# Where the bit patterns of the dense weights are put together: a PSUM bank in place of SBUF, for 16 of 32 pieces

## The chip, the cores and the metric

The kernel runs on one core of a Trainium2 chip. The metric is the device time of one execution in microseconds (us), as a median over runs. The engines have their own instruction streams and meet through semaphores: TensorE (PE in the profile, with its weight loads as PEld), VectorE (DVE), ScalarE (ACT), GpSimd (POOL) and SyncE (SP), which issues most DMAs. Working memory is SBUF; TensorE writes its results to PSUM, which has eight banks of 512 fp32 values in each of 128 partitions, and VectorE and ScalarE can read and write PSUM too.

## What is computed

Three layers follow each other. The first is attention over q, k and v of shape (4, 8, 768, 64), where each query sees the 4 first keys and a window of 128 keys:

```
scores = scale * q @ k.T                 # keep = sink | in_window, else -1e9
a = exp(scores - max); a = a / (sum(a) + 1e-9)
x = a @ v                                # -> 3072 tokens x 512
```

The second is a dense layer; w_in is 512 x 2048 and w_out 2048 x 512:

```
h = x @ w_in
g = where(h >= 1, h, where(h <= -1, 0, (h + 1)**2 / 4))
y = g @ w_out
```

The third routes the 3072 tokens of y to 8 experts with 384 places each, in the order of their gate logits, and gives each token its expert's `relu(y @ w1[e]) @ w2[e]`. The weights of the dense layer arrive as 64-bit floats, everything that the kernel multiplies is 32-bit.

## The kernel before, in words

**Splitting.** Matrix products take operands of type fp32r, with fewer mantissa bits than fp32. So each operand is split into a high part and a low part (names ending in h and l), and each product is three passes: low x high, high x low and high x high.

**Weights.** The two dense matrices come in 16 pieces each. Piece f of w_in holds columns 128f to 128f + 127, and piece f of w_out the same rows. A piece is a DMA of 512 KB into a tile dr (two of them), in which each weight is a pair of 32-bit words. `decode` (L230) turns a piece into fp32 and then into its two parts:

1. L237, ScalarE: the sign of the high word as plus or minus a power of two, written into the place of the low part.
2. L239, VectorE: bits of the low word, shifted, into the tile df; 128 x 512 elements.
3. L242, VectorE: the high word, shifted, combined with what L239 left in df.
4. L243, ScalarE: the absolute value, in place.
5. L244, VectorE: times the sign; df now holds the fp32 weights.
6. L245, ScalarE: the high part. L246, GpSimd: df minus the high part, the low part.

The tile df has three buffers in SBUF; pieces 12 to 15 of w_out use the pool tag "ev" instead, with two buffers that other tiles share. For w_out there are two more steps: `gate_t` (L210) transposes the piece on TensorE into a bank (gp), ScalarE copies it to SBUF (gw, L216), and `gate_m` (L218) multiplies it by the router's weights (gg), which ScalarE and VectorE split (L225, L226).

**Dense layer.** For a block of 256 tokens and each f, `hid` (L625) makes 128 hidden rows (hp), takes the activation over VectorE (L640, L642) and ScalarE (L641), and splits it into gh (ScalarE, L643) and gl (GpSimd, L644). `proj` multiplies both by piece f of w_out (up, L657). `hid` of f needs piece f of w_in, `proj` of f needs piece f of w_out with its gate part.

**PSUM.** Hidden rows use a tag H with two banks, the three sums of `proj` use U0, U1 and U2, and the tag A has two banks and R one. That makes eight. Transposes and scores ask `bank` (L179) for a bank; it goes round a list `free` of tags, which is A, A, R from plan time T0M on. So each third request gets the single bank R.

**Order.** `Plan` (L1340) collects steps, each with a time of the plan (about, but not exactly, microseconds), and then runs them in that order; this gives the instructions their priority, and the order on each engine is written when the program is built, by priority and by when inputs and buffers are expected to be free. The engines follow the written order. Pieces 0 to 6 of both matrices come at plan times 6 to 48; pieces 7 to 15 of w_in at D1 = 69 and every 2.79 after it; pieces 7 to 15 of w_out at 71.25 and every 4.5. The attention of block 2 begins at TA2 = 100. Blocks 0 and 1 of the dense layer, for which the weights must be decoded, run beside this.

Of the kernel before, what the change touches and what calls it, by code (L numbers as in the profile page):

```python
# [7 lines left out]
F32 = mybir.dt.float32  # L8
# [3 lines left out]
I32 = mybir.dt.int32  # L12
AF = mybir.ActivationFunctionType
OP = mybir.AluOpType
# [11 lines left out]
P = 128  # L26
# [19 lines left out]
H1, D0, DA, D1, DD = 7, 6.0, 6.5, 69.0, 4.5  # L46
# [5 lines left out]
TA2, TA3 = 100.0, 148.0  # L52
# [22 lines left out]
class Kernel:  # L75
# [154 lines left out]
    def decode(self, raw, oh, ol, late=False, pinned=False):  # L230

        nc = self.nc
        hw, lw = raw[:, :, :, 1], raw[:, :, :, 0]
        f = (self.mo if late else self.dec).tile([P, 4, P], F32, name="df", tag="ev" if late else "df", bufs=2 if late else 3)
        x, s = f.bitcast(I32), ol

        nc.scalar.activation(s, hw.bitcast(F32), AF.Sign, scale=2.0 ** -111 / 1.125)  # L237

        ins = nc.vector.tensor_scalar(x, lw, 29, 0x40000000, op0=OP.logical_shift_right, op1=OP.bitwise_xor)  # L239
        if pinned:  # L240
            self.tc.keep_in_program_order(ins)
        nc.vector.scalar_tensor_tensor(x, hw, 3, x, op0=OP.logical_shift_left, op1=OP.bitwise_xor)  # L242
        nc.scalar.activation(f, f, AF.Abs)  # L243
        nc.vector.tensor_tensor(out=f, in0=f, in1=s.bitcast(F32), op=OP.mult)  # L244
        nc.scalar.copy(oh, f)  # L245
        nc.gpsimd.tensor_tensor(out=ol, in0=f, in1=oh.bitcast(F32), op=OP.subtract)  # L246
        return f
# [1127 lines left out]
@with_exitstack  # L1375
def tile_sink_window_attention__moe__expert_choice(ctx, tc, q, k, v, n_sink, window, w_in, w_out, wg, w1, w2, out):
    a = dict(q=q, k=k, v=v, n_sink=n_sink, window=window, w_in=w_in, w_out=w_out, wg=wg, w1=w1, w2=w2, out=out)
    nc = tc.nc
    K = Kernel(ctx, tc, a)
    K.c = ctx.enter_context(tc.tile_pool(name="const", bufs=1))  # L1380
    dr = ctx.enter_context(tc.tile_pool(name="dr", bufs=1, space=DRAM))
    K.x2d = dr.tile([N, DM], F32, name="x2d")
    xg = dr.tile([B * H * S, D], F32, name="xg")
    K.logits = K.c.tile([P, B * NT, E], F32, name="logits")
    K.sk, K.sv, K.skf, K.svf = {}, {}, {}, {}

    def pipeline(general):
        with ExitStack() as c0:
            c1, c3, c4, cd = (c0.enter_context(ExitStack()) for _ in range(4))
            K.pools(c1.enter_context, c0.enter_context)  # L1390
            K.front_pools(c3.enter_context)
            K.dec = cd.enter_context(tc.tile_pool(name="dec", bufs=2, side="right"))
            if not general:
                K.consts()
            xs = {}
            gw, w_in, w_out, gate_t, gate_m = K.weight_steps()

            def xtiles(b):
                if b not in xs:
                    xs[b] = tuple(K.xp.tile([P, 4, TB], F32R, name=n, tag=n) for n in ("xh", "xl"))  # L1400
                return xs[b]

            def attn(plan, blks, t0, t1):
                if general:
                    for i, b in enumerate(blks):
                        plan.at(t0 + (t1 - t0) * i / len(blks), lambda b=b: K.load_x(b, xg, *xtiles(b)))
                    return
                steps = K.pipeline([p for b in blks for p in (K.attn_steps_f32 if b < NF else K.attn_steps)(b, xtiles)])
                dt = 1 / (len(steps) - 0.5)
                for i, s in enumerate(steps):  # L1410
                    plan.add(t0 + (t1 - t0) * dt * (i - 0.5 * (i > 0)), t0 + (t1 - t0) * dt * (i + 0.5), s)

            K.turn_, K.free = 0, ["U0", "A", "U1", "R", "U2", "A"]
            plan = Plan(tc)
            attn(plan, range(1), 0, T0A)
            attn(plan, range(1, 2), A1, B1)
            plan.at(T0M, lambda: setattr(K, "free", ["A", "A", "R"]))
            x01 = [xtiles(1), xtiles(0)]
            plan.add(T0M, T00, K.moe1_steps(0, lambda: xtiles(0), part=(0, H0)))
            plan.add(T1, T2, K.moe1_steps(1, lambda: xtiles(1)))  # L1420
            plan.add(T2, T3, K.moe1_steps(0, lambda: xtiles(0), part=(H0, FT)))
            plan.at(1, gw)
            if not general:
                plan.at(T0A, K.flags)

            def late():
                cd.close()
                K.late_weights(c1.enter_context)

            for f in range(FT):  # L1430
                t, TD = (D0 + f * DA, DA) if f < H1 else (D1 + (f - H1) * DD, DD)
                plan.at(t if f < H1 else D1 + (f - H1) * DD * WF, lambda f=f: w_in(f))
                if f == FA:
                    plan.at(t + TD / 2, late)
                plan.at(t + TD / 2, lambda f=f: w_out(f))
                plan.at(t + TD / 2 + TG, lambda f=f: gate_t(f))
                plan.at(t + TD / 2 + TG + (TH if f < FA - 1 else 1), lambda f=f: gate_m(f))

            def turn():
                c3.close()  # L1440
                K.router_pools(c0.enter_context)
                hold.append(c4.enter_context(tc.tile_pool(name="hold", bufs=1, side="right")))
                K.router_consts()
                K.rtag = "R"

            def clear():
                c4.close()
                c1.close()
                K.pools2(c0.enter_context)

            hold = []
            b1 = T3 + BLOCK * (NB - 3)
            attn(plan, range(2, 3), TA2, TA3)
            attn(plan, range(3, NB), TA3, b1 - BLOCK * AHEAD)
            for b in range(2, NB - 1):
                plan.add(T3 + BLOCK * (b - 2 - OV), T3 + BLOCK * (b - 1), K.moe1_steps(b, lambda b=b: xtiles(b)))
            plan.at(b1 - BLOCK * OV - 0.5, turn)
            to_logits, rest = K.moe1_steps(NB - 1, lambda: xtiles(NB - 1), lambda: hold[0])
            plan.add(b1 - BLOCK * OV, b1 + HB, to_logits)
            plan.add(b1 + HB, b1 + HB + TP, rest)  # L1460
            plan.at(b1 + HB + TP, clear)
            K.experts(plan, b1 + HB)
            plan.run()

    pipeline(False)
    flag = nc.values_load(K.flag[0:1, 0:1], min_val=0, max_val=1)
    with tc.If(flag):
        with ExitStack() as c0:
            K.attn_general(c0.enter_context, xg)
        pipeline(True)  # L1470
# [32 lines left out]
```

## Time and profile before

| | |
|---|---|
| median of 3 runs | 1175.04 us (1173.58 to 1175.45) |
| the profiled execution | 1172.83 us, of which the span from first to last instruction is 1171.0 |
| TensorE | 1102.2 us busy (94%), 8256 matmul records |
| weight loads of TensorE | 1017.4 us (87%) |
| VectorE | 872.2 us (74%) |
| ScalarE | 698.2 us (60%) |
| GpSimd | 487.0 us (42%) |
| mean granted TensorE clock | 0.982 of full speed |

"Busy" is the time in which an engine has an instruction running. A matmul's record overlaps the next one, so a busy TensorE is not TensorE at its peak. An idle time is put down to what released the waiting instruction, "<-"; it costs something only where the engine is the one that the end waits for. In the timeline rows a VectorE instruction's time overlaps its successor's by some 0.06 to 0.1 us.

### The profile page before, as it was taken

The numbers are of one execution on the slowest core, as the hardware profiler recorded it, in microseconds if no ns is written. First come the engines' busy times: TensorE is split into PE (matmuls) and PEld (weight loads), VectorE is DVE, ScalarE is ACT, GpSimd is POOL, SyncE is SP. The second block draws the span as 40 slices with busy tenths as digits, with TensorE's granted clock in tenths as the row PEclk, the third lists the DMA queues.
The fourth block names the chain that finished last, engine by engine and source line by source line (L and its number), as shares of the span: only waits on it lengthen the run. The fifth ranks groups of instructions, "written<-read, shape, count | busy, mean of one in ns | idle before, by whom it ended". The sixth has DMA issues, their size and how long they took to land.

```text
span 1171.0 us, 24367 instructions
## 1 busy us (share of the span) xinstructions
PE 1102.2 (94%) x8256; PEld 1017.4 (87%) x8256; DVE 872.2 (74%) x2718; ACT 698.2 (60%) x1598; POOL 487.0 (42%) x590
## 2 busy tenths in 40 slices
PE   5899888999999999999999999999799999999997
PEld 3688878999999999999999999999587788788896
DVE  5978978777777877776777787755788888788430
ACT  4887777566666666676667676643245445444552
POOL 1335745444545545455545554542213213322321
PEclk9899999999999999999999999999799999999999
DMA  4645522323222222223222222100485767667772
GB/s 105 173 143 158 158 60 61 70 42 64 53 39 56 36 55 49 61 46 64 34 54 49 58 46 56 22 19 1 120 228 168 204 180 216 188 194 202 217 218 66
DMA packets 241928, 118.13 MB, mean 101 GB/s; under 512 B 196096, under 2 KB 220672, under 8 KB 241792
## 3 DMA queue, kind: packets, MB, share of 16 engines
q1 hardware_dynamic: 231504, 85.36, 28.4%
q0 software_dynamic: 8592, 29.89, 10.9%
q8 instruction: 67, 1.10, 0.4%
q10 hardware_dynamic: 1696, 1.22, 0.3%
q14 instruction: 69, 0.57, 0.2%
HBM read 86.00 MB, written 13.11 MB: 85 GB/s over the span
## 4 chain that ended last, share of the span: by engine, by line
PE 42%; DVE 13%; issue 9%; ACT 6%; POOL 5%; DMA 4%; SPq 2%; DVEq 0%; POOLq 0%; ACTq 0%
PE hp L632 11%; PE up L657 11%; PE hp L1048 6%; PE us L1075 6%; PE xp L389 1%; DVE oh L945 1%; ACT pr L337 1%; ACT u L641 1%; PE tp L370 1%; SPq L424 1%; DVE u L640 1%; DVE ind L801 1%; DVE ks L301 1%; DMA qr<-in_q_dram 1%; POOL gl L644 1%
## 5 line engine op out<-in xcount | busy, mean ns | idle before, releaser
L644 POOL TENSOR_TENSOR gl<-u,gh 128x256 fp32r<-128x256 f32 x192 | 149.5, 779 | 205.3 <-ACT gh L643 169.5
L657 PE MATMUL up<-woh,gl 128*128 128x256 f32 x576 | 166.6, 289 | 2.6 <-POOL gl L644 2.6
L657 PE MATMUL up<-woh,gh 128*128 128x256 f32 x576 | 163.7, 284 | 0.0
L657 PE MATMUL up<-wol,gh 128*128 128x256 f32 x576 | 163.5, 284 | 0.0
L641 ACT ACTIVATE u<-u,half 128x256 f32<-128x256 f32 x192 | 97.4, 508 | 83.4 <-DVE u L640 79.4
L632 PE MATMUL hp<-xh,wil 128*128 128x256 f32 x768 | 132.0, 291 | 3.6 <-ACT xh L409 2.8
L632 PE MATMUL hp<-xl,wih 128*128 128x256 f32 x768 | 126.4, 284 | 2.0 <-POOL xl L410 1.6
L632 PE MATMUL hp<-xh,wih 128*128 128x256 f32 x768 | 124.7, 283 | 0.0
L632 PEld LDWEIGHTS hp<-xh,wil 128*128 128x128 f32 x768 | 107.6, 191 | 5.7 <-ACT xh L409 4.2
L657 PEld LDWEIGHTS up<-woh,gl 128*128 128x128 f32 x576 | 108.9, 189 | 3.2 <-POOL gl L644 3.1
L632 PEld LDWEIGHTS hp<-xl,wih 128*128 128x128 f32 x768 | 106.4, 191 | 3.4 <-POOL xl L410 3.4
L657 PEld LDWEIGHTS up<-wol,gh 128*128 128x128 f32 x576 | 108.6, 189 | 0.4 <-issue 0.4
L657 PEld LDWEIGHTS up<-woh,gh 128*128 128x128 f32 x576 | 108.5, 188 | 0.4 <-issue 0.4
L632 PEld LDWEIGHTS hp<-xh,wih 128*128 128x128 f32 x768 | 106.3, 191 | 0.0
L642 DVE TENSOR_TENSOR u<-hp,u 128x256 f32<-128x256 f32 x192 | 80.5, 420 | 31.6 <-ACT u L641 29.8
L640 DVE TENSOR_SCALAR u<-hp 128x256 f32<-128x256 f32 x192 | 79.9, 416 | 31.0 <-PE hp L632 22.5
L351 POOL TENSOR_TENSOR pr<-pr,sm 128x576 f32<-128x576 f32 x56 | 71.3, 1273 | 67.9 <-DVE sm L343 30.3
L643 ACT CAST gh<-u 128x256 fp32r<-128x256 f32 x192 | 77.6, 404 | 30.3 <-DVE u L642 28.0
L337 ACT ACTIVATE pr<-pr,sm 128x288 f32<-128x288 f32 (+1 forms) x160 | 85.2, 533 | 16.3 <-DVE sm L335 15.7
L1056 ACT ACTIVATE hh<-hp 128x384 fp32r<-128x384 f32 x64 | 31.5, 492 | 102.1 <-PE hp L1048 89.4
L373 DVE TENSOR_TENSOR pt<-tp,pt 128x512 fp32r<-128x512 f32 (+1 forms) x80 | 51.3, 647 | 43.9 <-ACT pt L372 43.4
L1075 PE MATMUL us<-w2h,hl 128*128 128x512 f32 x192 | 80.8, 421 | 0.0
(264 smaller groups left out, 3040.0 us busy)
## 6 DMA issues: line engine op xcount, KB each, us to landing
w1r<-in_moe_w_dram SPq DMA_DIRECT2D x32, 512.0 KB, 4.7
w2r<-in_moe_w_dram SPq DMA_DIRECT2D x32, 512.0 KB, 4.5
w2l<-w2r POOLq DMA_DIRECT2D x32, 512.0 KB
qr<-in_q_dram SPq DMA_DIRECT2D x320, 32.0 KB, 1.9
dr<-in_moe_w_in_dram SPq DMA_DIRECT2D x15, 512.0 KB, 4.1
dr<-in_moe_w_out_dram SPq DMA_DIRECT2D x15, 512.0 KB, 3.7
x2d<-ev SPq DMA_DIRECT2D x26, 256.0 KB, 2.2
vr<-in_v_dram SPq DMA_DIRECT2D x56, 96.0 KB, 2.3
```

Source lines behind the costliest of these rows:

```text
L337: nc.scalar.activation(pr, pr, AF.Exp, bias=sm[:, 0, u:u + 1], scale=-1.0, accum_out=sm[:, 1, u:u + 1])
L351: nc.gpsimd.tensor_tensor(out=pr, in0=pr, in1=r.unsqueeze(2).to_broadcast([P, 2, 2 * P + NS]), op=OP.mult)
L373: nc.vector.tensor_tensor(out=pt[:, 1, :n], in0=ps, in1=pt[:, 0, :n].bitcast(F32), op=OP.subtract)
L632: nc.tensor.matmul(ps, w_[:, k, fs], x_[:, k, :], start=(i == 0 and k == 0), stop=(i == 2 and k == 3))
L640: nc.vector.tensor_scalar(u, ps, -1.0, 1.0, op0=OP.max, op1=OP.min)
L641: nc.scalar.activation(u, u, AF.Square, bias=self.half, scale=0.5)
L642: nc.vector.tensor_tensor(out=u, in0=ps, in1=u, op=OP.max)
L643: nc.scalar.copy(gh, u)
L644: nc.gpsimd.tensor_tensor(out=gl, in0=u, in1=gh.bitcast(F32), op=OP.subtract)
L657: nc.tensor.matmul(o, g_[:, ts], self.w_out_part(w_, f)[:, cs], start=(f == fa and i == 0 and (cs.start > 0 or t == 0)), stop=(f == fz - 1 ...
L1048: nc.tensor.matmul(ps, w_[:, k, fs], x_[:, k, :], start=(i == 0 and k == 0), stop=(i == 2 and k == 3))
L1075: nc.tensor.matmul(us[j], h_[:, o], w_[:, f % 2, :], start=(f == 0 and i == 0), stop=(f == nf - 1 and i == 2))
```

## The change

In plan time from D1 - 0.1 to TA2 - 0.1 a flag `in_psum` is on. A decode that is traced in that time puts steps L239 to L243 into a PSUM bank of the tag R; L244 reads the bank and writes df, and what follows is as before. That holds for pieces 7 to 15 of w_in and 7 to 13 of w_out: 16 of 32 decodes. In the same time `free` is A, A, so that transposes, gate products and scores go round the two banks of A, and R serves the decodes alone, one at a time. Afterwards `free` is A, A, R again.

```diff
         f = (self.mo if late else self.dec).tile([P, 4, P], F32, name="df", ...)
-        x, s = f.bitcast(I32), ol
+        m = self.psum([P, 4, P], "R", "dx") if self.in_psum else f
+        x, s = m.bitcast(I32), ol
...
         nc.vector.scalar_tensor_tensor(x, hw, 3, x, op0=OP.logical_shift_left, op1=OP.bitwise_xor)
-        nc.scalar.activation(f, f, AF.Abs)
-        nc.vector.tensor_tensor(out=f, in0=f, in1=s.bitcast(F32), op=OP.mult)
+        nc.scalar.activation(m, m, AF.Abs)
+        nc.vector.tensor_tensor(out=f, in0=m, in1=s.bitcast(F32), op=OP.mult)
...
-            K.turn_, K.free = 0, ["U0", "A", "U1", "R", "U2", "A"]
+            K.turn_, K.free, K.in_psum = 0, ["U0", "A", "U1", "R", "U2", "A"], False
...
+            def decoding(on):
+                K.in_psum, K.free = on, ["A", "A"] if on else ["A", "A", "R"]
+
+            plan.at(D1 - 0.1, lambda: decoding(True))
+            plan.at(TA2 - 0.1, lambda: decoding(False))
```

## Rows read from the trace of the kernel before

**Rows 1.** The page's 40 slices of the span, busy tenths, TensorE.
```profile
PE   5899888999999999999999999999799999999997
```

**Rows 2.** Stretches: length, busy (x instructions) of PE, PEld, DVE, ACT, POOL, clock, DMA share, GB/s.
```profile
94.20:158.60 64.40, 57.11 (x456) 54.49 (x457) 56.64 (x104) 48.22 (x106) 40.60 (x35) 1.00 0.46 134
...
171.00:700.00 529.00, 508.36 (x4133) 501.80 (x4132) 406.99 (x1141) 356.70 (x912) 269.37 (x334) 0.99 0.26 52
```

**Rows 3.** Waits of TensorE, 94.2 to 158.6 us: total us, times, longest us.
```profile
PE gp L214 <- DVE df L244: 4.4, 5, 1.5
PE up L657 <- POOL gl L644: 2.6, 3, 1.7
PE gg L222 <- ACT gw L216: 0.5, 2, 0.3
```

**Rows 4.** Groups, 94.2 to 158.6 us, VectorE: busy us, mean ns | idle before.
```profile
L242 DVE SCALAR_TENSOR_TENSOR df<-dr,df 128x512 int32<-128x512 int32 x16 | 15.1, 946 | 0.1
...
L239 DVE TENSOR_SCALAR df<-dr 128x512 int32<-128x512 int32 x16 | 11.7, 730 | 1.9 <-POOL wql L246 1.4 <-POOL wil L246 0.4
...
L244 DVE TENSOR_TENSOR df<-df,wil 128x512 f32<-128x512 f32 x9 | 8.6, 952 | 1.6 <-ACT df L243 1.6
...
L640 DVE TENSOR_SCALAR u<-hp 128x256 f32<-128x256 f32 x15 | 6.2, 412 | 0.6 <-PE hp L632 0.6
...
L642 DVE TENSOR_TENSOR u<-hp,u 128x256 f32<-128x256 f32 x14 | 5.8, 415 | 0.3 <-ACT u L641 0.3
...
L244 DVE TENSOR_TENSOR df<-df,wol 128x512 f32<-128x512 f32 x6 | 5.4, 905 | 0.4 <-ACT df L243 0.4
...
L244 DVE TENSOR_TENSOR df<-df,wql 128x512 f32<-128x512 f32 x2 | 1.4, 693 | 1.6 <-ACT wql L237 1.6
```

**Rows 5.** The same view, GpSimd and ScalarE.
```profile
L644 POOL TENSOR_TENSOR gl<-u,gh 128x256 fp32r<-128x256 f32 x15 | 14.9, 995 | 2.5 <-issue 2.0 <-ACT gh L643 0.4
...
L243 ACT ACTIVATE df<-df 128x512 f32<-128x512 f32 x17 | 10.8, 633 | 6.1 <-DVE df L242 5.7 <-DVE wol L226 0.2
...
L216 ACT COPY gw<-gp 128x512 f32<-128x512 f32 x7 | 4.0, 577 | 0.0
```

**Rows 6.** Groups of the whole run, VectorE reading a bank, and gl.
```profile
L373 DVE TENSOR_TENSOR pt<-tp,pt 128x512 fp32r<-128x512 f32 x56 | 38.1, 688 | 32.1 <-ACT pt L372 31.7
...
L644 POOL TENSOR_TENSOR gl<-u,gh 128x256 fp32r<-128x256 f32 x192 | 149.5, 779 | 205.3 <-ACT gh L643 169.5
```

**Rows 7.** Timeline of VectorE, two steps with two SBUF inputs: start us, us.
```profile
103.52 1.51 DVE L301 TENSOR_TENSOR ks<-kr,ks 64x384 fp32r<-64x384 f32 x1
...
110.41 1.78 DVE L244 TENSOR_TENSOR df<-df,wil 128x512 f32<-128x512 f32 x1
```

**Rows 8.** Timeline of GpSimd beside the second of them.
```profile
109.90 1.74 POOL L246 TENSOR_TENSOR wil<-df,wih 128x512 fp32r<-128x512 f32 x1
```

**Rows 9.** Timeline, all engines: one L244 and the transposes behind it.
```profile
141.83 1.27 DVE L244 TENSOR_TENSOR df<-df,wol 128x512 f32<-128x512 f32 x1
...
143.15 0.66 PE L214 MATMUL gp<-ident,df 128*128 128x128 f32 x4 [1.03 <-DVE df L244]
```

**Rows 10.** Timeline of VectorE: decode steps of the first and the seventh decode.
```profile
94.51 0.88 DVE L239 TENSOR_SCALAR df<-dr 128x512 int32<-128x512 int32 x1 [0.42 <-POOL wil L246]
...
95.99 0.67 DVE L242 SCALAR_TENSOR_TENSOR df<-dr,df 128x512 int32<-128x512 int32 x1
96.70 0.43 DVE L239 TENSOR_SCALAR df<-dr 128x512 int32<-128x512 int32 x1
...
100.50 0.68 DVE L244 TENSOR_TENSOR df<-df,wil 128x512 f32<-128x512 f32 x1
...
120.08 1.67 DVE L242 SCALAR_TENSOR_TENSOR df<-dr,df 128x512 int32<-128x512 int32 x1
...
122.45 0.69 DVE L244 TENSOR_TENSOR df<-df,wil 128x512 f32<-128x512 f32 x1 [0.36 <-ACT df L243]
```

**Rows 11.** Waits of TensorE, 171 to 700 us, the longest in total.
```profile
PE tp L370 <- POOL pr L351: 12.0, 11, 2.0
```

## The prediction

> **What bounds the kernel now.** I read the page's slices first [rows 1]: TensorE is busy in nine tenths of almost every slice, so the end is set by how seldom TensorE stands still, and a change far ahead of the end is worth the TensorE waits it removes or adds. Then I placed the change in time: the sixteen decodes that it touches are the 15th to the 30th of 32 in the plan; their first L239 begins at 94.51 us [rows 10]. The stretch 94.2 to 158.6 us is therefore the one to read. [...]
>
> [...] In the groups by line [rows 4] the decode's VectorE steps take 730 ns (L239), 946 ns (L242) and 905 to 952 ns (most of L244). Steps that read a PSUM bank in the same stretch are not stretched: L640 412 ns and L642 415 ns. On GpSimd [rows 5] gl takes 995 ns against 779 ns over the whole run [rows 6]. The timeline shows what happens: L244 at 110.41 takes 1.78 us and ends at 112.19, 0.55 us after GpSimd's L246 that began at 109.90 and ended at 111.64 [rows 7, 8]. So a VectorE step with two SBUF inputs and a GpSimd step block each other. The trace pays for it on TensorE: the L244 at 141.83 takes 1.27 us, and the transposes at 143.15 stood 1.03 us for it [rows 9].
>
> [...]
>
> **The change, part by part.**
>
> *L239* (shift and xor, SBUF to bank): now 16 in 11.7 us [rows 4], 0.43 us when unhindered (96.70 [rows 10]). No row has VectorE writing a bank. Ends: 0.43 (nothing lost) and 0.73 (today's hindered mean). I take 0.69, the time of a 128x512 step that reads a bank (L373, 688 ns [rows 6]), because L640, half as wide and from a bank, takes 412 ns, and 256 more elements at L640-to-L373's slope (276 ns) lead there. 16 x 0.69 = 11.0 us, saving 0.7 us.
>
> *L242* (one input in SBUF, one in the bank, out to the bank): now 15.1 us. Ends 0.67 (95.99 [rows 10], unhindered) and 0.946; I take 0.69: 11.0 us, saving 4.1.
>
> *L244* (bank times sign, out to SBUF), the very form of L373: the rows give 8.6 + 5.4 + 1.4 = 15.4 us for 17, one of them (0.68) of an untouched decode, so 14.7 for sixteen; at 0.69 it is 11.0, saving 3.7.
>
> Sum on VectorE: 41.5 to 33.0, so 8.5 us less; its ends are -13 us (L239 at 0.43, the others at 0.67) and 0. VectorE then needs 48.1 of 64.4 us and has 16.3 us to spare where it had 7.8.
>
> [...]
>
> *L243* (Abs, now bank to bank): 633 ns in SBUF; the copy L216 that reads a bank takes 577 [rows 5]. Between 0 and 16 x 0.056 = 0.9 us less on ScalarE, which is off the path (48.22 of 64.4 us): counted as nothing.
>
> *GpSimd*: fewer blocks. gl could fall from 995 to 779 ns, 15 x 0.216 = 3.2 us less. Two-input steps of the attention in this stretch still block (L301 took 1.51 us at 103.52 [rows 7]), so I take half of it, 1.6 us.
>
> *New wait: one bank.* In the kernel before up to three decodes have a buffer; now the next L239 waits until the L244 before has read the bank. Behind it in VectorE's order stand L640, L642, L226, and so gh, gl and the gate weights. In six of the fifteen pairs the next L239 started before that (96.70 against 100.50 [rows 10]). Moving it leaves VectorE to stand while ScalarE makes the Abs. The time from the end of L242 to the start of L244 is at least 0.70 us (121.75 to 122.45) and 3.84 at the first (96.66 to 100.50); the sixteen sum to about 24 us [rows 10]. At the least gap, wholly unfilled, they cost 16 x 0.70 = 11.2 us, inside the 16.3 us to spare. So I cost it at 1 us of TensorE's time, with ends of 0 and 7.6 (below).
>
> *Two banks for gate transposes and products*: seven copies of gw in 64.4 us [rows 5], so fourteen holds. One of transposes lasts for them (0.66 us [rows 9]), the copy (0.58) and the waits between; at an estimate of 3 us each they fill 42 of 129 bank-us. Cost nothing; without that cover TensorE would stand up to 3 us once. The scores of block 2 get bank R again after the last of these decodes: between 0 and 3 us, taken as nothing, since that decode no longer waits for its SBUF buffer ahead of L239. DMAs and queues are not moved.
>
> *On the path.* Of the 4.4 us for L244 I take 3.6 as gone (four of five waits begin with a hindered step), of the 2.6 us for gl 1.4 (the longest, 1.7, lies behind that L301), less the 1.0 for the bank: 4.0 us. After 158 us TensorE is 96% busy (508.36 of 529 [rows 2]) with the same work in the same order, so an earlier start is kept; late next are the transposes that wait for GpSimd's normalization (12.0 us in 171 to 700 us [rows 11]), which start earlier by the same amount. The profiled execution took 1172.83 us, 1171.0 of it span, so it becomes 1168.8. The median of the runs is 2.2 us above it: 1175.04 - 4.0 = **1171.0 us**.
>
> **Rivals.**
>
> *The bank serializes the decodes* (slower). For it: one buffer, a chain of four steps over two engines, gaps of up to 3.84 us. Against it: 16.3 us to spare, and other VectorE work to put in the gaps. It decides from the point where more than 16.3 of the 24 us stay unfilled; with all of them VectorE needs 48.1 + 24 = 72.1 us, 7.6 more than the stretch has. About 5 us, 1180.
>
> *Waits only move* (no change). TensorE's order is written when the program is built, and other step times give another order. If the waits for L244 are replaced by waits for the two banks or for the block-2 attention's loads, under 2.3 us is left: 1174.5. For it: TensorE is already 89% busy here. Against: both named waits have a hindered producer.
>
> *All of it goes.* Every wait of [rows 3] vanishes, 7.3 us: 1167.7. Against it: L301 and the like still block.
>
> [...]
>
> **How the numbers follow.** About 0.2% (2.35 us) is what a measurement of this kernel can tell from no change. Forecast (2.4 to 6 us less) 0.47; all of it goes 0.10; waits only move 0.18; the lock is not left 0.08; the bank serializes 0.17. Faster: 0.57. Same: 0.18 + 0.08 = 0.26. Slower: 0.17. The range reaches from 1166 (all of it, and a little from better order) to 1179, short of the serializing case's far half.
>
> **What would show it.** Right: L239, L242, L244 each near 0.69 us for the sixteen with no row over 0.8, gl near 0.85, VectorE at some 48 us of the stretch, TensorE's waits for L244 under 1 us, and the first score of block 2 (154.38 now) 4 us earlier. Wrong: steps of over 1 us left among the sixteen; VectorE waiting for L243 sixteen times; a longer stretch; or the scores 4 us earlier and the end not, which would mean that the gain is given back by waits behind it.

## The result, and the profile after

The changed kernel is slower: 1180.76 us median (1179.51 to 1181.89, six runs) against 1173.67 us for the kernel before on the same chip, a ratio of 1.0056 [1.0046, 1.0066], 7.1 us more. The forecast was 1171.0 us, in a range of 1166 to 1179: wrong in sign. The time that came is the one given for the rival "the bank serializes the decodes" (1180). In the changed kernel the lines from L235 on stand one further down, and dx is a decode's tile in the bank: the decode's steps are now L240 (shift), L243 (combine), L244 (Abs), L245 (multiplication), L246 (ScalarE's copy) and L247 (GpSimd's subtraction).

The groups by line of VectorE, 94.2 to 171 us (line, engine, operation, names and shapes | busy us, mean ns of one | idle just before, and what ended it). The window is longer than that of [rows 4] because the sixteen decodes now end at 169 us:

```profile
L243 DVE SCALAR_TENSOR_TENSOR dx<-dr,dx 128x512 int32<-128x512 int32 x16 | 11.0, 689 | 0.2
L240 DVE TENSOR_SCALAR dx<-dr 128x512 int32<-128x512 int32 x16 | 11.0, 688 | 0.2
L641 DVE TENSOR_SCALAR u<-hp 128x256 f32<-128x256 f32 x17 | 7.1, 419 | 5.9 <-PE hp L633 4.4 <-POOL gl L645 1.4
...
L245 DVE TENSOR_TENSOR df<-dx,wil 128x512 f32<-128x512 f32 x9 | 6.2, 686 | 3.3 <-ACT dx L244 3.3
L245 DVE TENSOR_TENSOR df<-dx,wol 128x512 f32<-128x512 f32 x5 | 3.5, 692 | 3.2 <-ACT dx L244 3.2
...
L245 DVE TENSOR_TENSOR df<-dx,wql 128x512 f32<-128x512 f32 x2 | 1.4, 688 | 2.8 <-ACT dx L244 2.8
```

The steps themselves did exactly what was forecast: means of 688, 689 and 686 to 692 ns, and none of the 48 over 0.70 us. What is new stands in the last column: 9.3 us of VectorE standing for the Abs over the three groups of L245, and 4.4 us standing for TensorE (hp).

The stretches, in the columns of [rows 2], for the forecast's stretch, what is added to it, and the long stretch behind:

```profile
94.20:158.60 64.40, 56.03 (x419) 53.47 (x419) 45.97 (x92) 43.75 (x95) 32.73 (x34) 0.91 0.44 127
158.60:171.00 12.40, 11.84 (x78) 11.57 (x79) 7.49 (x21) 8.14 (x21) 4.12 (x4) 0.79 0.14 42
171.00:700.00 529.00, 505.13 (x4099) 497.05 (x4098) 411.09 (x1145) 357.11 (x916) 268.93 (x332) 0.99 0.27 53
```

TensorE runs 419 matmuls in the first stretch where it ran 456, and its granted clock is 0.91 in place of 1.00. All five busy times are lower there: no engine is busy throughout, they wait in turn. In steps of 10 us from 140 us on:

```profile
140.00:150.00 10.00, 8.16 (x43) 7.54 (x43) 5.62 (x11) 5.21 (x11) 4.07 (x5) 0.67 0.33 105
150.00:160.00 10.00, 5.65 (x28) 5.00 (x29) 4.61 (x9) 4.56 (x11) 3.92 (x4) 0.67 0.01 2
160.00:170.00 10.00, 9.83 (x67) 9.56 (x66) 6.49 (x21) 6.47 (x18) 3.07 (x3) 0.81 0.18 52
```

The first two steps in the kernel before:

```profile
140.00:150.00 10.00, 8.97 (x74) 8.57 (x73) 9.46 (x16) 7.06 (x15) 6.66 (x6) 1.00 0.29 79
150.00:160.00 10.00, 8.41 (x66) 7.60 (x65) 6.80 (x19) 7.18 (x19) 5.05 (x6) 1.00 0.17 54
```

Here the time goes: 71 matmuls from 140 to 160 us (140 before), at a granted clock of 0.67 in place of 1.00, and TensorE busy for only 5.65 us from 150 to 160. The waits of TensorE, 94.2 to 175 us (waiting line <- line waited for: us in total, times, longest):

```profile
PE hp L633 <- POOL wil L247: 4.0, 2, 2.6
PE up L658 <- POOL wol L247: 2.1, 2, 1.2
PE hp L633 <- DVE u L643: 1.4, 1, 1.4
PE gp L214 <- DVE df L245: 1.1, 2, 0.8
```

The wait for L245 fell from 4.4 us [rows 3] to 1.1 and the one for gl is gone, as forecast. In their place TensorE waits for finished weight pieces: 6.1 us for L247, the end of a decode, for which it did not wait once in the kernel before. The same waits on VectorE:

```profile
DVE df L245 <- ACT dx L244: 9.3, 11, 2.8
DVE u L641 <- PE hp L633: 4.4, 5, 2.6
DVE wol L226 <- ACT woh L225: 3.5, 2, 2.3
```

How the two tables hang together is seen in the chain of waits of 139 to 160 us (start us, us, what; each piece was released by the one above it):

```profile
143.00 1.23 POOL wil L247
144.23 0.04 issue
144.27 2.94 PE hp L633 x12
...
147.31 0.06 DVE u L641
147.37 0.28 issue
147.65 0.69 DVE dx L240
148.34 0.02 issue
148.37 0.71 DVE dx L243
149.07 0.02 issue
149.10 0.34 ACT dx L244
149.44 0.15 issue
149.59 0.66 ACT wil L238
150.25 0.30 ACT gh L644
...
150.69 0.73 POOL gl L645
151.42 1.25 POOL wol L247
152.67 0.04 issue
152.71 0.62 PE up L658 x3
```

It is a ring. GpSimd finishes a piece (144.23), TensorE can then make hp, VectorE's L641 takes hp (147.31), and behind L641 in VectorE's order stands the next shift (147.65), which begins the next decode, at whose end (152.67) TensorE again gets a piece. The multiplication of the decode before that shift had ended at 144.70. The timeline of VectorE:

```profile
144.01 0.69 DVE L245 TENSOR_TENSOR df<-dx,wil 128x512 f32<-128x512 f32 x1 [0.65 <-ACT dx L244]
147.31 0.43 DVE L641 TENSOR_SCALAR u<-hp 128x256 f32<-128x256 f32 x1 [2.61 <-PE hp L633]
147.65 0.68 DVE L240 TENSOR_SCALAR dx<-dr 128x512 int32<-128x512 int32 x1
```

And TensorE at the same time, one group of four hp matmuls, from 136.75, at a granted clock of 1.00 (136 to 138 us) and two, from 144.27, at 0.50 (144 to 150 us):

```profile
136.75 0.64 PE L633 MATMUL hp<-xh,wil 128*128 128x256 f32 x4
...
144.27 1.22 PE L633 MATMUL hp<-xh,wil 128*128 128x256 f32 x4 [1.39 <-POOL wil L247]
145.29 1.05 PE L633 MATMUL hp<-xl,wih 128*128 128x256 f32 x4
```

In the second of two gaps of TensorE, 0.91 us (before 140.20) and 1.39 us (before 144.27), the granted clock falls to 0.50 (0.90 from 143 to 143.5 us, 0.50 from 143.5); hp then takes 1.05 us per four in place of 0.64, and each turn of the ring takes longer. In this stretch of the kernel before it stayed at 1.00 [rows 2].

The sixteen decodes, from the end of the 14th decode's multiplication to the end of the 30th's subtraction on GpSimd, take 73.3 us; in the kernel before 63.6. Some 3.2 of these 9.7 us come at the start: the first shift goes at 97.75 us (94.51 [rows 10]). ScalarE's copy that frees a bank of transposes (L216) ends at 97.72; that this bank is R fits, but no view names it. The first score of block 2 moves from 154.41 to 165.50 us, and the end of the profiled execution by 7.5 (span 1178.5 against 1171.0).

### The profile page after: what moved, and what is told of

It reads as the page before. It is cut to its first block, busy times and chain, and to the rows that moved or that the text cites. A ratio compares the mean times of both kernels' runs of the same rounds, so it can differ in the third digit from the quotient of the medians.

```text
span 1178.5 us, 24377 instructions
## 1 busy us (share of the span) xinstructions
PE 1107.3 (94%) x8256; PEld 1021.3 (87%) x8256; DVE 867.2 (74%) x2718; ACT 697.3 (59%) x1598; POOL 480.9 (41%) x590
## 3 DMA queue, kind: packets, MB, share of 16 engines
q10 hardware_dynamic: 1696, 1.22, 0.3%
## 4 chain that ended last, share of the span: by engine, by line
PE 58%; DVE 14%; issue 9%; ACT 6%; POOL 5%; DMA 5%; SPq 1%; ACTq 0%; POOLq 0%; DVEq 0%
PE up L658 16%; PE hp L633 16%; PE hp L1049 6%; PE us L1076 6%; PE xp L390 2%; PE tp L371 2%; PE sc L333 1%; POOL pr L352 1%; PE sc L334 1%; DVE oh L946 1%; PE xp L572 1%; DVE ind L802 1%; DVE ks L302 1%; SPq L425 1%; POOL gl L645 1%
## 5 line engine op out<-in xcount | busy, mean ns | idle before, releaser
L645 POOL TENSOR_TENSOR gl<-u,gh 128x256 fp32r<-128x256 f32 x192 | 146.8, 765 | 200.5 <-ACT gh L644 168.2
L658 PE MATMUL up<-woh,gl 128*128 128x256 f32 (+1 forms) x576 | 166.9, 291 | 0.0
L658 PE MATMUL up<-wol,gh 128*128 128x256 f32 (+1 forms) x576 | 164.8, 286 | 2.1 <-POOL wol L247 2.1
L642 ACT ACTIVATE u<-u,half 128x256 f32<-128x256 f32 x192 | 97.4, 508 | 84.9 <-DVE u L641 81.0
L641 DVE TENSOR_SCALAR u<-hp 128x256 f32<-128x256 f32 x192 | 80.0, 417 | 37.7 <-PE hp L633 27.2
L643 DVE TENSOR_TENSOR u<-hp,u 128x256 f32<-128x256 f32 x192 | 80.6, 420 | 29.1 <-ACT u L642 27.5
```

The lines of the kernel that those rows point to most:

```text
L641: nc.vector.tensor_scalar(u, ps, -1.0, 1.0, op0=OP.max, op1=OP.min)
L642: nc.scalar.activation(u, u, AF.Square, bias=self.half, scale=0.5)
L643: nc.vector.tensor_tensor(out=u, in0=ps, in1=u, op=OP.max)
L645: nc.gpsimd.tensor_tensor(out=gl, in0=u, in1=gh.bitcast(F32), op=OP.subtract)
L658: nc.tensor.matmul(o, g_[:, ts], self.w_out_part(w_, f)[:, cs], start=(f == fa and i == 0 and (cs.start > 0 or t == 0)), stop=(f == fz - 1 ...
```

## Which half of the change costs

The first run gives the transposes and products two banks in the stretch, as the change does, and leaves the decodes in SBUF. The second gives the decodes a second place: R and a buffer of A in turn.

```diff
 e1_two_banks
-        m = self.psum([P, 4, P], "R", "dx") if self.in_psum else f
+        m = f
 e3_bank_RA
+        if self.in_psum:
+            self.dx_ = getattr(self, "dx_", 0) + 1
+        m = self.psum([P, 4, P], "RA"[self.dx_ % 2], "dx") if self.in_psum else f
```

Expected of the first: 

> One part alone: transposes and gate products go round the two banks of A in the stretch, the decodes stay in SBUF and bank R stands empty. Theory (the decodes queue for one bank, and that costs the 7 us): within 2 us of the kernel before, 1172 to 1176, and shift, combine and multiply still stretched (means near 0.73, 0.95, 0.92 us). Rival (two banks for transposes are too few): most of the 7 us, 1178 to 1182. Rival (any other written order does this): anything from 1170 to 1180.

Expected of the second: 

> The change, but the decodes go round R and A, so that a second one can begin while the first waits for its absolute value; transposes and gate products stay on the two banks of A. Theory (queue for one bank): over half of the loss is gone, 1169 to 1176, and the next shift starts before the multiplication in some pairs. Rival (two banks for transposes): A is now asked for more often, so 1181 or slower.

Two banks for the transposes: 1172.39 us, 0.9979 [0.9965, 0.9993]. They cost nothing. R and A in turn: 1166.76 us, 0.9929 [0.9910, 0.9949], faster than both kernels and 2 us below the range that was expected. Its stretch, in the columns of [rows 2], and the two waits of TensorE that answer to [rows 3] (its lines stand two further down than in the changed kernel):

```profile
94.20:158.60 64.40, 60.34 (x464) 58.25 (x464) 50.45 (x108) 49.89 (x110) 35.82 (x36) 0.95 0.48 136
```

```profile
PE gp L214 <- DVE df L247: 1.4, 1, 1.4
...
PE up L660 <- POOL gl L647: 0.8, 1, 0.8
```

TensorE is busy for 60.34 us of the stretch (57.11 before), and the wait for the multiplication is 1.4 us where it was 4.4. That is the gain the forecast spoke of, and more. So decodes in two places are worth about 7 us here, and a single place in their stead takes away 14 (1166.76 to 1180.76; 15 by the two ratios, each of which is to the kernel before as it ran beside that kernel).

## One place, shared or held for a shorter time

Four more ways to loosen the place: the transposes keep A, A, R beside decodes in R and A; only every second decode uses R; the combining step writes SBUF, so that R is held for two VectorE steps only; and R for shift and combine, with a buffer of A for Abs and multiplication.

```diff
 e6_RA_three (on e3_bank_RA)
-                K.in_psum, K.free = on, ["A", "A"] if on else ["A", "A", "R"]
+                K.in_psum, K.free = on, ["A", "A", "R"]
 e5_every_second
+        self.dx_ = getattr(self, "dx_", 0) + self.in_psum
+        m = self.psum([P, 4, P], "R", "dx") if self.in_psum and self.dx_ % 2 else f
 e4_short
-        nc.vector.scalar_tensor_tensor(x, hw, 3, x, ...)
-        nc.scalar.activation(m, m, AF.Abs)
-        nc.vector.tensor_tensor(out=f, in0=m, in1=s.bitcast(F32), op=OP.mult)
+        nc.vector.scalar_tensor_tensor(f.bitcast(I32), hw, 3, x, ...)
+        nc.scalar.activation(f, f, AF.Abs)
+        nc.vector.tensor_tensor(out=f, in0=f, in1=s.bitcast(F32), op=OP.mult)
 e7_split (its combining step as in e4_short, its multiplication as in the change)
-        nc.scalar.activation(m, m, AF.Abs)
+        if self.in_psum:
+            m = self.psum([P, 4, P], "A", "dy")
+        nc.scalar.activation(m, f, AF.Abs)
```

Expected of A, A, R: 

> Decodes alternate between bank R and a buffer of A, and the transposes and products keep A, A, R as in the kernel before. Theory: what cost time was a single bank for a chain of four steps; with two places the decodes overlap again, whoever else uses them. Now the bank R is shared with transposes, so a shift can wait for a transpose's copy (about 1 to 2 us in some of eight cases): 1166 to 1171 us, near the run with R and A in turn and the transposes on A, A (1166.8). Rival (the gain of that run came from keeping the transposes off bank R): 1174 us or more.

Expected of every second: 

> Only every second decode of the stretch uses bank R; the others stay in SBUF. Theory (the one bank is held from a shift to its multiplication, and the next shift is stuck behind other VectorE work that waits for TensorE): with an SBUF decode between two bank decodes the bank is back long before it is wanted, so the shift never waits for it. The eight decodes in the bank keep steps near 0.69 us, the eight in SBUF are stretched as before. Half of what the steps save (about 4 us of VectorE) is left, and the loss is gone: 1169 to 1174 us, below the kernel before or equal to it. Rival (any order of VectorE's instructions other than the one before costs, the bank itself is not the cause): near the changed kernel, 1177 to 1182 us.

Expected of the short hold: 

> The change, but the combine step writes its result to the SBUF tile, so the bank is held for two VectorE steps that can follow each other and not over ScalarE's absolute value; absolute value and multiplication are in SBUF as before. Theory (queue for one bank): the queue costs nothing, shift and combine near 0.69 us, multiplication stretched to 0.8 to 0.95; 1169 to 1175. Rival (two banks for transposes): 1179 to 1182 as with the change.

Expected of the split: 

> The shift writes bank R, the combining step reads it and writes SBUF, the Abs goes from SBUF into a buffer of A, and the multiplication reads that. Each bank is held over two neighbouring steps only, and no VectorE step has two SBUF inputs. Theory: the bank is free again right after the combining step, before ScalarE's Abs, so the next shift has no reason to wait, and the steps are as short as in the changed kernel: 1164 to 1170 us, as good as R and A in turn. Rival (the gain of R and A in turn came from a lucky order): 1172 us or more.

Measured: A, A, R 1172.43 us, 0.9994 [0.9982, 1.0007]; every second 1173.67 us, 1.0005 [0.9993, 1.0017]; short hold 1170.63 us, 0.9979 [0.9966, 0.9993]; split 1187.86 us, 1.0114 [1.0101, 1.0127]. None of the first three is slower than the kernel before, and each is 7 to 10 us faster than the changed one; A, A, R came out 1.4 us above what was expected, and with it the gain of two places is gone: it differs from R and A in turn only in that transposes use R too. One row of VectorE's waits (94.2 to 175 us) shows a price of that, a shift that waits for a transpose's copy to leave the bank; that this wait is all of it is not shown:

```profile
DVE dx L242 <- ACT gw L216: 3.6, 1, 3.6
```

The split is a miss by 18 us. Its sixteen decodes end only 3.1 us later than before; the loss comes behind them, at the last two decodes, which stay in SBUF and which the change does not touch. From the timeline of VectorE, and the waits of TensorE at 160 to 215 us:

```profile
166.84 0.43 DVE L240 TENSOR_SCALAR df<-dr 128x512 int32<-128x512 int32 x1
...
185.31 0.40 DVE L240 TENSOR_SCALAR df<-dr 128x512 int32<-128x512 int32 x1
```

```profile
PE gp L214 <- DVE df L247: 5.5, 2, 4.3
```

The two shifts are 18.5 us apart (6.9 in the kernel before). In between stand L643, L645 and steps of attention in VectorE's order, which wait for ScalarE and TensorE, once for 2.9 us; then TensorE stands 4.3 us for the last multiplication. Why the order puts that shift so late was not found. This is a case that the cause below does not cover.

## The order alone, with no place short

The kernel is a written order: once it is built, each engine runs its list. So the single bank can act in two ways: as a wait on the chip, or by the order that it forces when the program is built, in which a shift can only follow the multiplication before it. The next four runs put that order in by hand. In two, decodes go to R and A in turn, so that no place is short; in two they stay in SBUF. In each pair the shift is tied first to the multiplication before it, directly behind which it can be written (AFTER fixes the written order alone), and then to ScalarE's copy behind that, which is about 0.7 us later, so that another VectorE instruction gets in between, as it does in the changed kernel (DEP is a wait on the chip as well).

```diff
 e10_RA_chain (on e3_bank_RA), e2_sbuf_chain (on SBUF, transposes on A, A, R)
+        if self.in_psum and getattr(self, "mul", None):
+            self.tc.add_manual_dep(ins.ins, self.mul, AFTER, reason="one at a time")
...
-        nc.vector.tensor_tensor(out=f, in0=m, in1=s.bitcast(F32), op=OP.mult)
+        mul = nc.vector.tensor_tensor(out=f, in0=m, in1=s.bitcast(F32), op=OP.mult)
+        self.mul = mul.ins.name if self.in_psum else None
 e13_RA_cast (on e3_bank_RA), e14_sbuf_cast (on e1_two_banks): DEP in place of AFTER, and
-        nc.scalar.copy(oh, f)
+        mul = nc.scalar.copy(oh, f)
+        self.mul = mul.ins.name if self.in_psum else None
```

Expected in SBUF, behind the multiplication: 

> The queueing alone, without PSUM: the sixteen decodes stay in SBUF with three buffers and banks A, A, R, but each shift (first VectorE step) is written behind the multiplication (last VectorE step) of the decode before it. Theory (one decode at a time costs the 7 us): at least 5 us slower than before, 1179 to 1186, worse than the change if the blocked steps are still worth anything, and a granted clock under 0.9 somewhere between 140 and 170 us. Rival (two banks for transposes): as before, 1172 to 1176. Rival (PSUM steps themselves): as before.

Expected with R and A, behind the multiplication: 

> As the run with R and A in turn (1166.8 us), but each shift is written on VectorE behind the multiplication of the decode before it, mostly directly behind; no buffer is short. Theory (what costs time is that the decodes go one after another, through the written order, not any wait for a bank on the chip): the overlap is gone and with it most of the gain, but the shift still follows its multiplication at once: chain of decodes 65 to 70 us long instead of 59.7, time 1170 to 1176 us. Rival (two places gain by something else, as bank A being held less by transposes): it stays at 1165 to 1169 us.

Expected with R and A, behind the copy: 

> As the run with R and A in turn, but each shift waits for ScalarE's copy of the decode before it, so that it comes about 0.7 us later than its multiplication and one other VectorE instruction stands between, as the single bank makes it in the changed kernel; the bank itself is never short. Theory (the loss of the change is the lateness of the next shift and what gets between, not the bank as such): the chain becomes 70 us or longer and the time 1177 to 1183 us, like the changed kernel. Rival (the bank itself, or the transposes without R, cost the time): 1167 to 1174 us.

Expected in SBUF, behind the copy: 

> All decodes in SBUF, transposes and products on A, A as in the changed kernel, and each shift waits for ScalarE's copy of the decode before it, as in the run with R and A. Theory: late shifts cost the time whatever the decodes are written to, and the hindered steps come on top: 1178 to 1186 us, chain of 70 us or longer. Rival (only PSUM decodes are touched by it, since the SBUF chain with the shift at once took 1173.2 us): 1171 to 1175 us.

| kernel | place of the decodes | a shift before the multiplication ahead of it | decodes, us | time, us | ratio to before |
|---|---|---|---|---|---|
| before | 3 in SBUF | 6 of 15 | 63.6 | 1173.7 | |
| R and A in turn | 2 | 7 | 59.7 | 1166.8 | 0.9929 [0.9910, 0.9949] |
| short hold | 1, held briefly | 11 | 61.7 | 1170.6 | 0.9979 [0.9966, 0.9993] |
| changed | 1 | 0 | 73.3 | 1180.8 | 1.0056 [1.0046, 1.0066] |
| SBUF, tied to the multiplication | 3 | 0 | 68.6 | 1173.2 | 0.9996 [0.9982, 1.0009] |
| R and A, tied to the multiplication | 2 | 0 | 71.6 | 1183.1 | 1.0071 [1.0054, 1.0089] |
| R and A, tied to the copy | 2 | 0 | 81.6 | 1192.4 | 1.0153 [1.0137, 1.0169] |
| SBUF, tied to the copy | 3 | 0 | 84.4 | 1193.5 | 1.0165 [1.0150, 1.0180] |

("Decodes" is the time as measured above for the changed kernel; the third column counts the fifteen pairs in which a shift began over 0.2 us before the multiplication ahead of it had ended, both from the timeline of one profiled execution of each kernel. That of the SBUF run tied to the multiplication took 1176.4 us, more than its median.)

In R and A tied to the multiplication no place is short. The view of its shifts has no wait for a bank, only one for the pieces themselves:

```profile
its engine sat idle before it (us, times) until:
  DMA dr<-in_moe_w_in_dram: 1.7, 2
```

So the written order alone turns 1166.8 into 1183.1 us, a little worse than the change and far worse than was expected (1170 to 1176). With the later tie it is 1192.4 (1177 to 1183 expected), and in SBUF 1193.5 (up to 1186 expected); these two hold the shift up on the chip besides, for 3.8 us in R and A. One decode after another, with late shifts, thus costs as much as the bank does, without a bank that is short.

It does not cost so much everywhere. The SBUF run tied to the multiplication is a miss: 1173.2 where at least 5 us of loss had been expected, although its decodes take 5 us longer and its granted clock falls to 0.66 from 150 to 160 us. It differs from the run with R and A tied in the same way by the place of the decodes and by its transposes, which kept A, A, R; which of the two saves it no run shows. Decodes that took 5 us longer were still covered there; 70 us or more were covered in no run. In R and A tied to the copy, the stretch and the waits of VectorE (94.2 to 175 us) show the changed kernel's pattern, stronger:

```profile
94.20:158.60 64.40, 54.13 (x389) 52.16 (x389) 42.70 (x84) 41.49 (x88) 29.69 (x30) 0.86 0.46 130
```

```profile
DVE df L249 <- ACT dx L248: 9.5, 11, 2.3
DVE u L646 <- PE hp L638: 8.2, 6, 2.5
```

389 matmuls in the stretch (456 before), 9.5 us for the Abs and 8.2 us for hp: the ring again. In SBUF tied to the copy the steps were stretched besides, the combining step to a mean of 1432 ns (946 [rows 4]).

## A head start, and the accident of the order

If the chain is late, an earlier plan should help. Two runs move the plan of these decodes by 4 us (D1, the planned start of the first of them, from 69 to 65); in the first a 17th decode falls into the part with the bank, in the second it is kept out.

```diff
 e8_lead, e12_lead16
-H1, D0, DA, D1, DD = 7, 6.0, 6.5, 69.0, 4.5
+H1, D0, DA, D1, DD = 7, 6.0, 6.5, 65.0, 4.5
 e12_lead16 besides
+        self.dx_ = getattr(self, "dx_", 0) + self.in_psum
+        m = self.psum([P, 4, P], "R", "dx") if self.in_psum and self.dx_ <= 16 else f
```

Expected with 17 decodes: 

> The changed kernel with the decodes of the stretch planned to begin 4 us earlier (D1 65 in place of 69); one bank as in the change. Theory: the chain of decodes runs about 10 us late at its end, and the scores of block 2 and the transposes stand for it; a head start of at most 4 us gives back 2 to 5 us of that: 1176 to 1179 us, still slower than before. Rival (the lost time is not the lateness of the chain but the low granted clock that came by chance of order): any time between 1166 and 1182, with a clock of 0.95 or more from 140 to 160 us and yet a late chain.

Expected with sixteen: 

> The changed kernel with the decodes planned 4 us earlier (D1 65 in place of 69), and only the same sixteen in bank R. In the run with D1 65 alone (1185.1 us) a 17th decode took the bank too and the first score of block 2, which needs R, came 15 us later than before. Theory (the scores of block 2 stand for the bank, and the chain sets when it is back): with sixteen the bank is back some 6 us earlier than there, at or before its time in the changed kernel: 1175 to 1180 us. Rival (earlier decodes crowd VectorE and that made the loss): 1183 us or more again.

Both missed: 1185.07 us, 1.0098 [1.0083, 1.0112], and 1189.60 us, 1.0133 [1.0118, 1.0148]. The head start does not reach the end of the chain. With sixteen (in a profiled execution of 1182.9 us, well under its median), decodes take 73.2 us, as with D1 69, and the first score of block 2 comes at 167.83 us (165.50 in the changed kernel); with 17 it comes at 170.80. So it is not the plan that makes the decodes late; that it is the ring fits, but is argued from the changed kernel's trace.

But these misses and the split left open how much is the accident of one order, since each edit writes the whole order anew. So the kernel before, the changed kernel and R and A in turn were run with D1 at 68 and 67 (in the last two with sixteen decodes in PSUM each time).

```diff
-H1, D0, DA, D1, DD = 7, 6.0, 6.5, 69.0, 4.5
+H1, D0, DA, D1, DD = 7, 6.0, 6.5, 68.0, 4.5
```

Expected at 68, before: 

> The kernel before with the decodes of the stretch planned 1 us earlier (D1 68 in place of 69), which writes another order with the same parts. Theory (the accident of the order is small beside the bank's effect): within 4 us of the kernel before, 1170 to 1178 us. Rival (accident decides): anything, 1165 to 1190 us.

Changed: 

> The changed kernel with the decodes planned 1 us earlier, still sixteen in the bank. Theory (one place makes the decodes go one after another in every such order): 1177 us or more, as with D1 69 (1180.8), 65 (1185.1 and 1189.6). Rival (accident): it may come out below the kernel before.

R and A: 

> R and A in turn with the decodes planned 1 us earlier. Theory (two places let the decodes overlap in every such order): 1164 to 1172 us, below the kernel before. Rival (the 1166.8 us were an accident of one order): 1174 us or more.

Expected at 67, before: 

> The kernel before with the decodes of the stretch planned 2 us earlier (D1 67). Theory (the accident of the order is small): 1169 to 1178 us. Rival (accident decides): anything, 1165 to 1190 us.

Changed: 

> The changed kernel with the decodes planned 2 us earlier, sixteen in the bank. Theory (one place is slow in every order): 1177 us or more. Rival (accident): it may come out below the kernel before.

R and A: 

> R and A in turn with the decodes planned 2 us earlier. Theory (two places are fast in every order): 1163 to 1172 us, below the kernel before. Rival (accident): 1174 us or more.

| D1 | before | changed | R and A in turn |
|---|---|---|---|
| 69 | 1173.7 | 1180.8, 1.0056 [1.0046, 1.0066] | 1166.8, 0.9929 [0.9910, 0.9949] |
| 68 | 1176.0, 1.0023 [1.0010, 1.0036] | 1183.8, 1.0085 [1.0072, 1.0098] | 1169.8, 0.9967 [0.9957, 0.9977] |
| 67 | 1178.1, 1.0045 [1.0030, 1.0060] | 1187.5, 1.0109 [1.0094, 1.0124] | 1166.9, 0.9934 [0.9920, 0.9948] |

(Ratios are to the unmoved kernel before.) All six times lie in the ranges of the theory, the kernel before at 67 at its edge. The medians of the three groups never overlap: at the same D1, one place is 7 to 9.5 us slower than the kernel before, and two places are 6 to 11 us faster. Another order moves a group by 3 to 7 us and turns no sign. It fits with the miss of the head start too: from 69 to 67 each us of an earlier plan costs the kernel before some 2 us and the changed kernel some 3.

## Why the prediction was wrong, point by point

- **L240, L243, L245 at 0.69 us each**: right, means of 688, 689 and 686 to 692 ns; 33.1 us for the 48 by the rows, as summed. L245, which reads a bank, took no longer (686 to 692 ns) than the two in the kernel before with both inputs in SBUF and unhindered (693 [rows 4]). Nor did a GpSimd step beside them stretch the 48: 666 to 697 ns for all, beside a GpSimd busy for 32.73 of 64.4 us. Nine L243 ran wholly beside an L247, as at 124.14 beside the one from 123.91 (1.30 us), and took 0.67 to 0.70 us, where L244 at 110.41 took 1.78 us beside L246 [rows 7, 8]; L247 took 1.26 to 1.30 us, that L246 1.74. So the steps did not stay at 41.5 us, the case to which 0.08 was given as "the lock is not left" (1176 us).
- **Abs and GpSimd**: both came out as forecast or better, 583 ns for the Abs (633 [rows 5]) and 736 ns for gl (995 [rows 5]), where 0.85 us had been forecast. From the groups of 94.2 to 158.6 us:

```profile
L645 POOL TENSOR_TENSOR gl<-u,gh 128x256 fp32r<-128x256 f32 x16 | 11.8, 736 | 12.0 <-ACT gh L644 8.8 <-issue 2.9 <-POOL gl L645 0.3
...
L244 ACT ACTIVATE dx<-dx 128x512 f32<-128x512 f32 x14 | 8.2, 583 | 2.5 <-DVE dx L243 2.5
```

- **Two banks for transposes and products, at nothing**: right (1172.39 us).
- **On the path, -3.6 and -1.4** (of the 4.4 and 2.6 us of [rows 3]; in all TensorE was idle for 7.3 of 64.4 us [rows 2]): the two waits fell about as forecast, to 1.1 us and to none. But there TensorE stood for other things first; the clearer reading is R and A in turn, 1.4 and 0.8 us, so -3.0 and -1.8. With two places the whole was worth -7 us, more than the -5.0 that the forecast had without its term for the bank.
- **New wait: one bank, +1.0**: this step failed. The end of its range was 7.6 us (7.7 by its own terms). Against two places it measured 14.0 us (1180.76 - 1166.76): the gain of about 7 us was lost, and 7.1 us more. The step weighed gaps of 24 us against VectorE's 16.3 us to spare, as if the bank could cost only VectorE's time. Neither was the limit: VectorE stood 9.3 us for the Abs, well under 16.3, and was busy for only 45.97 us of the stretch. The rival's own condition (over 16.3 us unfilled) was not met either; that its time came true was luck. Of the signs of being wrong a longer stretch came, and VectorE waited for the Abs eleven times.
- **What should have been counted** is the hold. From each L239's start to the end of its L244 the sixteen decodes of the kernel before take 73.7 us in sum, by the timeline rows of which [rows 10] shows two decodes, and they lie in 62.9 us (94.5 to 157.4), because they overlap. At these lengths one place cannot hold them in that time. In the changed kernel the holds sum to 61.8 us and the gaps between a multiplication and the next shift to 7.5; together, 69.3 us, they are all of the time from 97.75 to 167.12. The bank was held for 89% of it, and no view of the profile has a row for that. The holds of the changed kernel, 61.8 us, would by themselves have fitted into 62.9: what the sum shows is that nothing is left for a late start (3.2 us) and for gaps (7.5).
- **What is queued behind** was named in the forecast (L640, L642, L226) only as what a waiting shift would hold up. It went the other way too: those instructions, written ahead of the shift, wait for TensorE, which waits for the decode.
- **After 158 us**: "an earlier start is kept" held for the loss only in part. The first score of block 2 came 11.1 us late; of that some 5 us were left at 290 to 470 us, by the starts of the same instructions in both timelines. From 535 us to the end it was 7.2: in between, at 500 to 510 us, the granted clock of the changed kernel was 0.83 (1.00 before). So some 2 of the 7 us in these two executions arose far behind the stretch; why is not shown.

Open: how much of the loss the lower clock adds. It shows in every run of over 1180 us (0.86 to 0.95 from 94.2 to 158.6 us), but also, at 0.66 from 150 to 160 us, in R and A in turn and in the SBUF run tied to the multiplication, neither of which was slower than the kernel before. No run held it apart from the gaps beside it. Open too is the order of the split.

## What to carry to other kernels

A buffer that several engines hold in turn is a resource like an engine: before moving work into a single one, sum the holds from first write to last read in the trace of before and compare them with the stretch they must fit in (here 73.7 against 62.9 us); the spare time of the engines did not show it (VectorE was busy for 45.97 of 64.4 us). This sum was made after the result and was tried on no other kernel; it warns, but does not give the loss: the SBUF run tied to the multiplication had its decodes one after another and lost nothing. In the written order the shared place here also tied otherwise independent work into one list (none of the fifteen shifts came before the multiplication ahead of it), and as something in that list waited for the consumer of the work (L641 for hp, 4.4 us), a ring closed. Two places, taken in turn and one of them kept free of transposes, kept the gain of the shorter steps: 1166.8 us, the best version found here.

## What the runs showed of the hardware

- The VectorE steps that write a bank took one duration, with one SBUF input (L240, a mean of 688 ns) or one in each (L243, 689 ns): the shift, unhindered, took 0.43 us from SBUF to SBUF [rows 10] and 683 to 697 ns into the bank. The move paid only because the steps were hindered before (means of 730, 946 and 905 to 952 ns [rows 4]): unhindered, all three were as short or shorter in SBUF (0.43, 0.67 and 0.68 us [rows 10]).
- ScalarE's Abs from bank to bank took 583 ns, against 633 in SBUF [rows 5].
- Read in windows of 2 us, the granted clock of the changed kernel was at 0.50 from 144 to 150 and from 154 to 162 us. The first fall, at some 143.4 us, came in the second of two gaps of TensorE (0.91 and 1.39 us), the other, between 153.5 and 154 us, 0.8 us or more after the second of two (0.79 and 1.22 us); in the second stretch there is another gap, of 2.58 us. What makes the clock fall no run shows. Groups of four matmuls took 1.05 us there in place of 0.64.
